# Hash attention with adapters: the sum of v written once per head and added by VectorE

## The chip, the cores and the metric

The kernel runs on one core of one Trainium2 chip. Its metric is the device time of one execution in microseconds (us). The parts of the core that matter here are TensorE (PE, with PEld for its weight loads), VectorE (DVE), ScalarE (ACT), GpSimd (POOL) and the DMA queue that SyncE (SP) issues.

## The reference

Four batches of eight heads, 768 positions, head size 64. Queries and keys are hashed to six sign bits each; a key takes part for a query only where the two hashes agree. The heads' outputs, side by side, are 3072 rows of 512, on which a mixture of eight rank-16 adapters works.

```python
q_bits = (np.einsum('bhsd,dk->bhsk', q, proj) > 0)      # k likewise
mask = q_bucket[:, :, :, None] == k_bucket[:, :, None, :]
scores = np.where(mask, scale * q @ k.T, -1e9)          # scale = 1/8
attn = softmax(scores)                                  # no key agrees: all weights equal
x = (attn @ v)                                          # [4*768, 8*64]
logits = x @ w_gate                                     # two largest of 8 experts, softmax of these
out = x + sum over the two of w * (x @ A[e]) @ B[e]
```

Where no key agrees, softmax gives every key the same weight, so the output is the mean of v.

## The kernel before

The 32 heads are handled as 16 pairs (p = 0 to 15; two heads h). For each pair:

- q, k and v are loaded by SP (`load_q`, `load_k`, L176; `load_v`, L184) in natural layout, 128 partitions with six positions each.
- Hashes: VectorE turns 32x32 blocks (`turn32`, L212), TensorE multiplies by the hash weights (`hash`, L222), VectorE takes signs (`sign`, L231), and the signs go out to DRAM and come back as rows 64 to 71 of the tile aug (`sign_out`, L238; `sign_in`, L244).
- q and k proper: GpSimd scales and casts to bf16 (`natcast`, L252), a transposing DMA writes them into aug (`cross`, L259), and the second head's half is moved to the first partitions by VectorE for q and by GpSimd for k (`shift_v`, `shift_p`, L267).
- Scores: `s0` to `s8` (L365) are nine blocks of 1024 columns, keys in the partitions. The hash rows make scores of keys that don't agree so small that their exponential vanishes. There are three score banks (`ps_s`, `bufs=3`). ScalarE takes the exponential of each block (`x0` to `x8`, L371), 144 in all.
- Values: for each head, `p00` to `p05` and `p10` to `p15` (`pvk`, L384) multiply the exponentials by v with a column of ones beside it, into one bank (`ps_v`, `bufs=1`): six query tiles of 65 columns, the 65th being the sum of the weights. Ahead of them `u0` and `u1` (`uni`, L376) write the sum of v over all keys, multiplied by 2^-56, into all six tiles at once, 390 columns. This is the case in which no key agrees: beside real weights it is too small to count. GpSimd makes the sums of v over a partition's six positions in three steps (`vsum0` to `vsum2`, L200, L203, L205), the matmul sums over partitions.
- `norm0` and `norm1` (L401, L403): VectorE takes the reciprocal of each tile's 65th column and multiplies the 64 others by it, from the bank into x. When it has done so the bank is free for the next head.

Per batch (four pairs) x is cast (`to_bf`, POOL, L412), turned by TensorE (`turn`, L421), copied (`xcopy`, DVE, L426), and multiplied by the gate and the A matrices (`lz`, L443; copy `lzc`, DVE, L447); routing (`route`, `exp`, `gate`, `inv`) is small work on VectorE and ScalarE (L459 to L485), the products with the gate are on GpSimd (`prod`, L492), then come a turn (`zt`, `ztc`), the product with B (`d`, L518), the sum (`sum`, DVE, L536) and the store (`st`). Hashes, turns, gates and deltas share a single bank "m" (`ps_m`, `bufs=1`), so each of them waits until the one before has been copied out.

All orders are written out by hand: `PLAN` holds a row of steps for each pair, and every engine and the DMA queue executes its instructions in the order in which the steps stand. A step's suffix is the pair it belongs to, relative to the row: `hash+2` works ahead for a later pair, `norm1-1` finishes the pair before. In row 0 the first pair has special steps for its shorter start (`order`, `tr`, `copy`, `cast`, `hash`, `sign` by halves). The last two pairs are finished by other functions (`uni3`, `pv3`, `norm3`; steps with A to F), with their own broadcast matmul (L812).

Of the kernel before, what the change touches and what calls it, by code (L numbers as in the profile page):

```python
# [13 lines left out]
F32 = mybir.dt.float32  # L14
BF16 = mybir.dt.bfloat16
AX = mybir.AxisListType
ALU = mybir.AluOpType
# [3 lines left out]
class Emitter:  # L21
    def __init__(self, ctx, tc, q, k, v, proj, w_gate, A, Bm, out):
        self.tc, self.nc = tc, tc.nc
        self.q, self.k, self.v, self.out = q, k, v, out
        B, H, S, D = q.shape
# [38 lines left out]
        self.vs3, self.vs1, self.ps = {}, {}, {}  # L64
# [129 lines left out]
    def vsum(self, p, k):  # L194

        nc, T, D = self.nc, self.T, self.D
        vn, vb = self.vn[p], self.vb[p % 3]
        if k == 0:
            s3 = self.vs3[p] = self.vsp.tile([self.P, 2, 3, D], F32, tag="vs3", name=f"vs3_{p}")
            nc.gpsimd.tensor_add(out=s3, in0=vn[:, :, 0:3, :], in1=vn[:, :, 3:6, :])  # L200
        elif k == 1:
            s1 = self.vs1[p] = self.vsp.tile([self.P, 2, D], F32, tag="vs1", name=f"vs1_{p}")
            nc.gpsimd.tensor_add(out=s1, in0=self.vs3[p][:, :, 0, :], in1=self.vs3[p][:, :, 1, :])  # L203
        else:
            nc.gpsimd.tensor_add(out=vb[:, :, T, 0:D], in0=self.vs1[p], in1=self.vs3[p][:, :, 2, :])  # L205
# [167 lines left out]
    def uni(self, p, h):  # L373
        T, D = self.T, self.D
        pv = self.pv[p, h] = self.ps_v.tile([self.P, T, D + 1], F32, tag="v", name=f"pv{p}_{h}")
        self.nc.tensor.matmul(out=pv, lhsT=self.eps,  # L376
                              rhs=self.vb[p % 3][:, h, T:T + 1, :].to_broadcast([self.P, T, D + 1]),
                              start=True, stop=False, skip_group_check=True)
# [14 lines left out]
    def norm(self, p, h):  # L393
# [5 lines left out]
        pv = self.pv[p, h]  # L399
        ri = self.smallp.tile([P, T], F32, tag="ri", name=f"ri{p}_{h}")  # L400
# [290 lines left out]
    def step(self, token, p):  # L691
# [21 lines left out]

# [4 lines left out]

# [4 lines left out]

# [4 lines left out]

# [6 lines left out]

# [5 lines left out]

# [5 lines left out]

# [5 lines left out]

# [4 lines left out]

# [5 lines left out]

# [5 lines left out]

# [4 lines left out]

# [143 lines left out]
```

## Time and profile before

| what | us |
| --- | --- |
| runs | 160.62, 161.14, 164.03; median 161.14 |
| profiled execution, its own time | 161.96 |
| its span | 160.0 |
| PE busy / weight loads | 149.8 / 106.4 |
| ACT busy, of which the 144 exponentials | 140.1 / 134.2 |
| DVE busy | 115.1 |
| POOL busy | 109.0 |
| first exponential starts, last ends | 10.9, 148.4 |

The profile comes from one execution, whose own time lies between the runs; the span is what its instructions cover. Busy time of an engine is time in which at least one of its instructions runs, so instructions that overlap count once. A stretch A:B lies between two times from the span's start; its row gives the busy time of each engine, with the number of instructions in brackets, then the granted TensorE clock, the DMA share and GB/s. In a row of a group the figures behind the count are the busy time of all, the mean of one in ns, and the idle time of the engine before them with what ended it. In the order of time a row has its start, its length and what it is.

### The profile page before, as it was taken

What the parts mean: (1) busy time and instruction counts of PE and PEld (TensorE: products, weight loads), DVE (VectorE), ACT (ScalarE), POOL (GpSimd) and SP (SyncE); (2) the same over time, 40 slices, a digit from 0 to 9 for tenths busy, and PEclk for the clock granted to TensorE, in tenths of its full rate; (3) what the DMA queues carried; (4) which work ended last, traced back from release to release, by engine and by line L of the source; (5) the groups of instructions that cost most, each with busy time, mean ns of one, the idle gap of its engine ahead of it and who ended that gap; (6) DMA issues with size and microseconds to landing.
All of it is one profiled execution on the core that took longest, in us unless ns stands there. A gap on an engine that the chain in (4) does not pass through costs nothing.

```text
span 160.0 us, 5374 instructions
## 1 busy us (share of the span) xinstructions
PE 149.8 (94%) x2188; PEld 106.4 (66%) x2188; DVE 115.1 (72%) x316; ACT 140.1 (88%) x164; POOL 109.0 (68%) x180
## 2 busy tenths in 40 slices
PE   7999899999999999999999999999999999999730
PEld 4655566767676577666767776666777688899400
DVE  4488866477374779967768997778796777778861
ACT  3149989999999899999999999999999999998440
POOL 3489887975896947999989559996769359100360
PEclk9999999999999999999999999999999999999996
DMA  5898998989989989998989989899975552223146
GB/s 137 260 336 236 204 227 199 266 169 265 200 91 296 169 169 319 294 192 204 267 261 264 286 195 234 223 213 249 277 219 103 158 214 106 94 90 132 46 177 216
DMA packets 57552, 33.03 MB, mean 206 GB/s; under 512 B 42552, under 2 KB 55608, under 8 KB 57528
## 3 DMA queue, kind: packets, MB, share of 16 engines
q1 hardware_dynamic: 57304, 32.56, 82.3%
q8 instruction: 17, 0.28, 0.8%
q10 hardware_dynamic: 224, 0.13, 0.3%
q14 instruction: 7, 0.06, 0.1%
HBM read 20.15 MB, written 7.03 MB: 170 GB/s over the span
## 4 chain that ended last, share of the span: by engine, by line
PE 70%; DMA 15%; SPq 5%; DVE 3%; ACT 2%; issue 1%; POOL 1%; DVEq 0%; POOLq 0%
PE s L365 28%; PE pv L384 13%; DMA aug<-nb 11%; PE hs L222 5%; DMA nat<-in_k_dram 4%; PE lz L443 3%; PE pvl L822 3%; PE dl L518 2%; PE xtp L421 2%; PE pv L376 2%; SPq L147 2%; PE hb L582 2%; PE s L315 2%; PE xt L845 1%; ACT P L371 1%
## 5 line engine op out<-in xcount | busy, mean ns | idle before, releaser
L371 ACT ACTIVATE P<-s 128x1024 bf16<-128x1024 f32 x144 | 134.2, 1072 | 4.8 <-PE s L365 2.4
L365 PE MATMUL s<-aug 71*128 71x256 bf16 (+3 forms) x396 | 76.7, 311 | 0.2 <-DMA aug<-dr 0.2
L384 PEld LDWEIGHTS <-P 128*128 128x128 bf16 x1008 | 40.3, 98 | 9.1 <-issue 0.5
L384 PE MATMUL pv<-vb,P 128*128 128x65 bf16 x1008 | 43.4, 193 | 0.0
L365 PEld LDWEIGHTS <-aug 71*128 71x128 bf16 x396 | 31.9, 97 | 14.5 <-issue 3.3
L212 DVE STREAM_TRANSPOSE R<-nat 128x768 f32<-128x768 f32 x30 | 28.9, 968 | 1.8 <-DMA nat<-in_k_dram 1.6
L252 POOL TENSOR_SCALAR nb<-nat 128x768 bf16<-128x768 f32 x30 | 24.9, 831 | 2.5
L492 POOL TENSOR_TENSOR zm<-lzs,gw 128x128 bf16<-128x128 f32 x22 | 8.3, 402 | 20.3 <-DVE gw L478 18.2
L200 POOL TENSOR_TENSOR vs<-vn 128x384 f32<-128x384 f32 x16 | 16.0, 998 | 2.2 <-DMA vn<-in_v_dram 1.8
L536 DVE SCALAR_TENSOR_TENSOR acc<-dl,rt,x 128x512 f32<-128x512 f32 x18 | 13.4, 744 | 5.2 <-PE dl L518 5.2
L403 DVE TENSOR_TENSOR x<-pv,ri 128x384 f32<-128x384 f32 x28 | 15.6, 557 | 1.0
L412 POOL CAST xb<-x 128x768 bf16<-128x768 f32 x14 | 11.5, 824 | 6.4 <-DVE x L403 6.2
L267 POOL COPY aug<-aug 64x768 bf16<-64x768 bf16 x14 | 11.8, 843 | 4.4 <-DMA aug<-nb 3.8
L222 PE MATMUL hs<-R,hst 128*32 128x192 f32 x240 | 13.8, 332 | 0.2 <-DVE R L212 0.2
L192 POOL CAST vb<-vn 128x768 bf16<-128x768 f32 x16 | 13.4, 836 | 0.8 <-DMA vn<-in_v_dram 0.7
L401 DVE RECIPROCAL ri<-pv 128x6 f32<-128x6 f32 x28 | 5.3, 189 | 7.9 <-PE pv L384 7.5
L267 DVE COPY aug<-aug 64x768 bf16<-64x768 bf16 x14 | 8.8, 627 | 2.5 <-DMA aug<-nb 2.1
L222 PEld LDWEIGHTS hs<-R,hst 128*32 128x32 f32 x240 | 6.5, 109 | 5.4 <-DVE ri L401 1.8
L231 DVE TENSOR_SCALAR s<-hs,soff 128x192 bf16<-128x192 f32 x15 | 6.1, 410 | 5.0 <-PE hs L222 5.0
L443 PE MATMUL lz<-wa,xT 128*128 128x136 bf16 x96 | 9.5, 222 | 0.2 <-DVE xT L850 0.2
L376 PE MATMUL pv<-vb,eps 128*128 128x390 bf16 x28 | 9.3, 333 | 0.3 <-DVE aug L568 0.3
L426 DVE COPY xT<-xtp 128x768 bf16<-128x768 bf16 x14 | 7.7, 552 | 1.9 <-PE xtp L421 1.9
(98 smaller groups left out, 153.8 us busy)
## 6 DMA issues: line engine op xcount, KB each, us to landing
vn<-in_v_dram SPq DMA_DIRECT2D x16, 384.0 KB
nat<-in_q_dram SPq DMA_DIRECT2D x15, 384.0 KB
nat<-in_k_dram SPq DMA_DIRECT2D x15, 384.0 KB
out_dram<-acc SPq DMA_DIRECT2D x9, 512.0 KB
out_dram<-acc SPq DMA_DIRECT2D x5, 256.0 KB
dr<-s SPq DMA_DIRECT2D x15, 48.0 KB
aug<-dr SPq DMA_DIRECT2D x15, 48.0 KB
nat<-in_q_dram SPq DMA_DIRECT2D x2, 192.0 KB
```

The source lines that it names most:

```text
L192: nc.gpsimd.tensor_copy(out=vb[:, :, 0:T, 0:D], in_=vn)
L200: nc.gpsimd.tensor_add(out=s3, in0=vn[:, :, 0:3, :], in1=vn[:, :, 3:6, :])
L212: self.nc.vector.transpose(out=self.R[p][:, i], in_=self.nat[p][:, i])
L222: nc.tensor.matmul(out=self.hs[p][32 * j:32 * j + 32], lhsT=self.hst[:, hf].rearrange("p b i -> p (b i)"), rhs=rhs, start=(hf == 0), stop= ...
L252: self.nc.gpsimd.tensor_scalar(out=self.nb[p][:, :, i].rearrange("p t h d -> p h t d"), in0=self.nat[p][:, i].rearrange("p h (t d) -> p h ...
L267: (self.nc.gpsimd if i else self.nc.vector).tensor_copy(out=aug[0:64, :, i, 1, :], in_=aug[64:128, :, i, 0, :])
L365: nc.tensor.matmul(out=ps[:, c - lo:c - lo + n * P], lhsT=aug[0:71, kt, 1, h, :], rhs=aug[0:71, q:q + n, 0, h, :], start=True, stop=True)
L371: self.nc.scalar.activation(out=self.P_[p][:, lo:lo + 1024], in_=ps, func=ACT.Exp, scale=128.0)
L384: self.nc.tensor.matmul(out=pv[:, i, :], lhsT=self.P_[w][:, o:o + self.P], rhs=vb[:, h, kt, :], start=False, stop=(kt == self.T - 1), skip ...
L403: nc.vector.tensor_tensor(out=self.x[b][:, :, c:c + D], in0=pv[:, :, 0:D], in1=ri.unsqueeze(2).to_broadcast([P, T, D]), op=ALU.mult)
L443: nc.tensor.matmul(out=ps, lhsT=self.xT[b][:, t, i, :], rhs=self.wa[:, t, :], start=(t == 0 and (keep or i == I[0])), stop=(t == self.nD - ...
L536: nc.vector.scalar_tensor_tensor(out=acc, in0=ps, scalar=rt, in1=x, op0=ALU.mult, op1=ALU.add)
```

## The change

`uni` writes the scaled sum of v only once, as a seventh tile of 65 columns in the bank. `norm` copies these 65 columns to SBUF (um), adds them to the six tiles with one VectorE instruction into an SBUF tile (w), and takes reciprocal and multiply from that tile. The second step of the sum of v works in place. All 16 rows of `PLAN` differ; of these the first and two of the middle are shown.

```diff
@@ vsum
         elif k == 1:
-            s1 = self.vs1[p] = self.vsp.tile([self.P, 2, D], F32, tag="vs1", name=f"vs1_{p}")
-            nc.gpsimd.tensor_add(out=s1, in0=self.vs3[p][:, :, 0, :], in1=self.vs3[p][:, :, 1, :])
+            s3 = self.vs3[p]
+            nc.gpsimd.tensor_add(out=s3[:, :, 0, :], in0=s3[:, :, 0, :], in1=s3[:, :, 1, :])
         else:
-            nc.gpsimd.tensor_add(out=vb[:, :, T, 0:D], in0=self.vs1[p], in1=self.vs3[p][:, :, 2, :])
+            nc.gpsimd.tensor_add(out=vb[:, :, T, 0:D], in0=self.vs3[p][:, :, 0, :], in1=self.vs3[p][:, :, 2, :])
@@ uni
-        pv = self.pv[p, h] = self.ps_v.tile([self.P, T, D + 1], F32, tag="v", name=f"pv{p}_{h}")
-        self.nc.tensor.matmul(out=pv, lhsT=self.eps,
-                              rhs=self.vb[p % 3][:, h, T:T + 1, :].to_broadcast([self.P, T, D + 1]),
-                              start=True, stop=False, skip_group_check=True)
+        pv = self.pv[p, h] = self.ps_v.tile([self.P, T + 1, D + 1], F32, tag="v", name=f"pv{p}_{h}")
+        self.nc.tensor.matmul(out=pv[:, T, :], lhsT=self.eps, rhs=self.vb[p % 3][:, h, T, :],
+                              start=True, stop=True, skip_group_check=True)
@@ norm
         pv = self.pv[p, h]
+        um = self.smallp.tile([P, 1, D + 1], F32, tag="um", name=f"um{p}_{h}")
+        nc.vector.tensor_copy(out=um, in_=pv[:, T:T + 1, :])
+        w = self.vsp.tile([P, T, D + 1], F32, tag="pvs", name=f"pvs{p}_{h}")
+        nc.vector.tensor_tensor(out=w, in0=pv[:, 0:T, :], in1=um.to_broadcast([P, T, D + 1]), op=ALU.add)
+        pv = w
         ri = self.smallp.tile([P, T], F32, tag="ri", name=f"ri{p}_{h}")
         nc.vector.reciprocal(out=ri, in_=pv[:, :, D])
@@ PLAN, row 0
-        "order_q0 tr_q0 order_k0 copy_q0 tr_k0 warm4 proj_second order_k1 cast_q0 hash_q0 copy_k0 hash_k0 "
-        "load_q+1 order_q1 load_k+1 sign_q0 tr_q1 cast_k0 load_v sign_k0 copy_q1 tr_k1 copy_k1 load_q+2 "
-        "hash_q1 proj_groups turn32_q+1 cast_q1 hash_weights cast_k1 natcast_q+1 hash_k1 load_k+2 vcast "
-        "sign_q1 turn32_k+1 natcast_q+2 sign_k1 s0 natcast_k+1 s1 hash+1 s2 natcast_k+2 x0 sign+1 "
+        "order_q0 order_k0 tr_q0 copy_q0 tr_k0 cast_q0 load_q+1 proj_second copy_k0 hash_q0 hash_k0 "
+        "order_k1 sign_k0 load_k+1 order_q1 proj_groups cast_k0 sign_q0 tr_k1 copy_k1 tr_q1 hash_k1 "
+        "hash_weights copy_q1 natcast_q+1 hash_q1 load_k+2 load_q+3 cast_k1 s0 turn32_q+1 natcast_k+2 "
+        "sign_k1 sign_q1 x0 s1 cast_q1 load_v turn32_k+1 x1 s2 natcast_k+1 hash+1 load_q+2 t1q s3 sign+1 "
+        "load_k+3 turn32_k+2 q1q0 q1q1 x2 vcast s5 turn32_q+2 warm4 natcast_q+2 t1k vsum0 s4 x3 q1k1 s6 "
...
@@ PLAN, rows 5 and 6, new
+        "s0 lzc1:0 norm0-1 hash+2 sign+2 u1-1 p10-1 p11-1 x7-1 s1 shift_v+1 lz0:0 x0 x8-1 vsum2 lzc0:0 "
+        "p12-1 x1 p13-1 load_q+3 route0:0 p14-1 vsum0+1 p15-1 vsum1+1 exp0:0 lz3:0 s2 s3 vcast+1 "
+        "shift_p+1 s4 cross+2 lzc3:0 x2 norm1-1 u0 lz4:0 p00 lzc4:0 x3 p01 p02 sign_in+1 lz5:0 s5 "
+        "load_k+3 lzc5:0 to_bf-1 route1:0 s6 x4 shift_v+2 load_moe:5 exp1:0 gate1:0 gate0:0 x5 x6 turn-1 "
+        "p03 p04 sign_out+2 prod2:0 s7 prod0:0 inv1:0 p05 prod1:0 inv0:0 vsum2+1 load_k+4 x7 s8 xcopy-1 "
+        "load_v+2 norm0 x8",
+        "s0 zt0:0 load_q+3 u1-1 s1 cast_moe:5 ztc0:0 shift_p+1 d0:0 p10-1 load_v+2 sign_in+1 turn32_q+2 "
+        "x1 sum0:0 turn32_k+2 p11-1 p12-1 p13-1 s2 x0 p14-1 p15-1 x2 load_k+4 natcast_q+2 s3 natcast_k+2 "
+        "prod5:0 s4 prod3:0 cross+2 norm1-1 vcast+1 x3 hash+2 s5 natcast_k+3 u0 p00 p01 x4 prod4:0 p02 "
+        "natcast_q+3 sign+2 vsum0+1 turn32_q+3 d2:0 sum2:0 s6 turn32_k+3 s7 p03 d1:0 x5 s8 sign_out+2 "
+        "sum1:0 p04 p05 norm0 to_bf-1 x6",
```

More of the change, by code (lines that the diff above doesn't have):

```diff
@@ L63, in __init__ @@
         self.zm, self.zT, self.rt, self.acc, self.rg = {}, {}, {}, {}, {}
-        self.vs3, self.vs1, self.ps = {}, {}, {}
+        self.vs3, self.ps = {}, {}
         self.pend, self.at = {}, {}
```

146 rows, old and new, of the table PLAN are left out of this document.

## The prediction

> **What bounds the kernel now.** I read the page's first part, then a table of busy time by stretch, cut at the pairs of heads: before the first exponential, pairs 0 to 4, pairs 5 to 13, pairs 14 and 15, and the end behind the last exponential.
>
> ```profile
> span 160.0 us, 5374 instructions
> PE 149.8 (94%) x2188; PEld 106.4 (66%) x2188; DVE 115.1 (72%) x316; ACT 140.1 (88%) x164; POOL 109.0 (68%) x180
> ...
> core 0: us, PE busy (x) PEld busy (x) DVE busy (x) ACT busy (x) POOL busy (x), PEclk, DMA share, GB/s
> 0.00:10.90 10.90, 9.54 (x48) 6.05 (x50) 5.82 (x26) 2.82 (x5) 5.70 (x28) 1.00 0.77 232
> 10.90:54.63 43.73, 42.73 (x655) 28.53 (x652) 28.93 (x53) 41.85 (x45) 35.86 (x52) 1.00 1.03 215
> 54.63:130.40 75.77, 75.77 (x1159) 54.20 (x1158) 60.23 (x166) 75.23 (x86) 59.27 (x88) 1.00 0.92 224
> 130.40:148.42 18.02, 18.02 (x309) 15.72 (x306) 13.91 (x48) 17.35 (x21) 4.82 (x10) 1.00 0.35 139
> 148.42:160.00 11.58, 3.76 (x32) 1.89 (x30) 6.25 (x26) 2.87 (x9) 3.35 (x5) 0.87 0.38 138
> ```
>
> The shares of the whole span would name PE. The stretches say more: between 10.90 and 148.42 us ScalarE (ACT) is as full as PE, 75.23 of 75.77 us in the longest one. VectorE (DVE) has 60.23 there, the only compute engine with real room beside GpSimd (POOL). Next, how regular the exponentials are, from the order of time on ACT:
>
> ```profile
> 10.90 1.94 ACT L371 ACTIVATE P<-s 128x1024 bf16<-128x1024 f32 x2 [1.81 <-PE s L315]
> ...
> 20.45 8.39 ACT L371 ACTIVATE P<-s 128x1024 bf16<-128x1024 f32 x9 [0.80 <-PE s L365]
> ...
> 61.43 11.10 ACT L371 ACTIVATE P<-s 128x1024 bf16<-128x1024 f32 x12
> ```
>
> Twelve exponentials in a row take 11.10 us and one lasts 1.07 us (the group's row below), so they start (11.10 − 1.07)/11 = 0.91 us apart. All 144 at that pace need 143 × 0.91 + 1.07 = 131.2 us; they took 148.42 − 10.90 = 137.5. So the exponentials set a floor, and no relief of another engine can win back more than about 6 us between them. PE is level with ACT, and the score banks (three of them) let it run about two exponentials, 1.8 us, ahead.
>
> The Trainium skill says the same against reading PE's 94% as the bound: "Trainium Kernel Development and Optimization", section Performance Expectations, calls matmul busy time a bad measure because matmuls are pipelined and takes the weight loads' share for a better one. Here that is PEld's 66%.
>
> **The change part by part.** The prices come from the groups kept apart by shape (busy us, mean ns of one, then the idle time before them).
>
> ```profile
> L371 ACT ACTIVATE P<-s 128x1024 bf16<-128x1024 f32 x144 | 134.2, 1072 | 4.8 <-PE s L365 2.4 <-PE s L315 2.0
> L376 PE MATMUL pv<-vb,eps 128*128 128x390 bf16 x28 | 9.3, 333 | 0.3 <-DVE aug L568 0.3
> L812 PE MATMUL pvl<-vb,eps 128*128 128x65 bf16 x4 | 0.4, 193 | 0.0
> L403 DVE TENSOR_TENSOR x<-pv,ri 128x384 f32<-128x384 f32 x28 | 15.6, 557 | 1.0
> L401 DVE RECIPROCAL ri<-pv 128x6 f32<-128x6 f32 x28 | 5.3, 189 | 7.9 <-PE pv L384 7.5
> L447 DVE COPY lzs<-lz 128x136 f32<-128x136 f32 x18 | 5.3, 294 | 5.0 <-PE lz L443 4.9
> L459 DVE MAX8 top<-lzs 128x8 f32<-128x8 f32 x23 | 2.3, 155 | 0.1
> L485 DVE RECIPROCAL rt<-ss 128x3 f32<-128x3 f32 x7 | 1.2, 169 | 0.1
> L267 DVE COPY aug<-aug 64x768 bf16<-64x768 bf16 x14 | 8.8, 627 | 2.5 <-DMA aug<-nb 2.1
> L203 POOL TENSOR_TENSOR vs<-vs 128x128 f32<-128x128 f32 x16 | 7.3, 455 | 1.2
> ```
>
> *PE, removed.* The 390-column matmul with the small weights becomes one of 65 columns. That form stands in the trace (L812): 193 ns against 333. So 28 × 0.14 = 3.9 us of PE go. In the long stretch ACT is as full, so this buys slack, not time; in all I credit 0.5 us (bounds 0 and 3.9).
>
> *DVE, added.* Each of 28 head steps gets a copy of 65 columns and an addition of 390 before the reciprocal. The copy lies between L485's 169 ns (3 elements) and L447's 294 (136 columns): 0.22. The addition is L403's shape with six more elements: 0.56. Two instructions that depend on each other stand about 0.04 apart:
>
> ```profile
> 21.55 0.18 DVE L401 RECIPROCAL ri<-pv 128x6 f32<-128x6 f32 x1
> 21.77 0.56 DVE L403 TENSOR_TENSOR x<-pv,ri 128x384 f32<-128x384 f32 x1
> ```
>
> (21.55 + 0.18 = 21.73, and the multiply starts at 21.77.) So a head step costs 0.22 + 0.56 + 2 × 0.03 to 0.04 = 0.84 us more; at the ends, 0.17 + 0.56 + 0.06 = 0.79 and 0.30 + 0.56 + 0.08 = 0.94. The bank of a head is held no longer than now: copy and addition, 0.82 us, stand where reciprocal and multiply, 0.78, stood. Reciprocal and multiply now run behind the release, but on the same engine.
>
> *The multiply changes its place of reading.* It read the matmul's bank and ri; now both inputs lie in SBUF. The trace shows what such instructions meet when POOL works:
>
> ```profile
> 26.66 0.82 POOL L267 COPY aug<-aug 64x768 bf16<-64x768 bf16 x1 [0.81 <-DMA aug<-nb]
> 26.67 1.03 DVE L267 COPY aug<-aug 64x768 bf16<-64x768 bf16 x1
> ...
> 59.49 0.35 DVE L267 COPY aug<-aug 64x768 bf16<-64x768 bf16 x1
> ...
> 93.70 0.22 DVE L478 SCALAR_TENSOR_TENSOR gw<-lzs,top,e 128x8 f32<-128x8 f32 x1
> ...
> 93.85 0.44 DVE L478 SCALAR_TENSOR_TENSOR gw<-lzs,top,e 128x8 f32<-128x8 f32 x1
> 93.87 0.40 POOL L492 TENSOR_TENSOR zm<-lzs,gw 128x128 bf16<-128x128 f32 x1 [0.20 <-DVE gw L478]
> ```
>
> The same DVE copy took 0.35 us while POOL stood idle and 1.03 beside a POOL instruction that started 10 ns earlier: it ended 0.22 us behind it. The gate instruction (L478), with two tensor inputs in SBUF, took 0.22 us alone and 0.44 beside POOL's product. Over its 14 instances the copy averages 627 ns, 0.27 us above 0.35. I take 0.27 us for each multiply as well; the bounds are nothing (POOL never in the way) and 0.8 (a whole POOL instruction ahead). With it a head step costs 0.84 + 0.27 = 1.11 us more, 28 of them 31 us.
>
> The Trainium skill has the rule: "SBUF — State Buffer", section Who interferes with whom, says a VectorE instruction with two SBUF inputs contends with a GpSimd instruction that reads SBUF, whichever starts first keeping the shared ports to its end. The copy at 26.67 agrees for its kind. A reader who trusts only the opposite, that the multiply never waits, gets 0.84 per step.
>
> *What the sum is where it falls.* In the new lists rows 5 to 13 hold 19 head steps against 17 in the old; a head step costs 0.78 now. So DVE needs 60.23 + 2 × 0.78 + 19 × 1.11 = 82.9 us where the stretch lasts 75.77. Part of a busy figure overlaps when DVE is crowded: two transposes of 0.97 us fit in 1.91 (below), 0.03 less; the 23 maxima (L459) of 155 ns are busy 2.3 us together, 0.05 less on each. At 0.04 us on each of the 166 instructions, an estimate, 6.6 us go and 76.3 are left.
>
> ```profile
> 15.11 1.91 DVE L212 STREAM_TRANSPOSE R<-nat 128x768 f32<-128x768 f32 x2
> ...
> 88.22:96.86 8.64, 8.64 (x131) 6.28 (x130) 8.31 (x35) 8.56 (x12) 5.11 (x10) 1.00 0.94 248
> ```
>
> The most crowded pair of the old kernel had DVE busy for 8.31 of 8.64 us (96%). With every gap closed the stretch takes 76.3 us, +0.5; with 82.9 at 96% it takes 86.4, +10.6. I take the middle, **+5.5 us**. What queues behind a late multiply is everything DVE does for PE's one shared bank "m": signs (L231), turned copies (L426), gate copies (L447) and sums (L536). PE executes in order, so a hash, turn or delta that waits for that bank holds the next scores, and 1.8 us later ACT is idle.
>
> Pairs 0 to 4 have room: 28.93 + 8 × 1.11 = 37.8 of 43.73 us, though rows 1 and 2 of the new lists crowd; +0.5. Pairs 14 and 15 finish through the other helper (uni3, norm3), which is untouched, and the end as well: 0.
>
> *The first row of steps.* Four warming matmuls move from ahead of the first scores to behind the sixth, and the casts of the second halves are rearranged. The first exponential may come up to 0.9 us earlier. But pair 1 starts when its signs have gone out to DRAM and back:
>
> ```profile
> 12.52 0.42 DVE L231 TENSOR_SCALAR s<-hs,soff 128x192 bf16<-128x192 f32 x1 [0.45 <-PE hs L222]
> 12.96 0.37 SPq L238 DMA_DIRECT2D dr<-s  x1
> ...
> 16.66 0.34 SPq L244 DMA_DIRECT2D aug<-dr  x1
> ...
> 19.80 1.09 PEld L365 LDWEIGHTS <-aug 71*128 71x128 bf16 x8 [0.37 <-DMA aug<-dr]
> ```
>
> Sign at 12.52, out at 12.96, in at 16.66, first scores at 19.80: 7.3 us. In the new list pair 1's second transpose stands behind both late signs of pair 0, so this chain does not start earlier. An earlier first exponential waits longer at 20.45 (it waits 0.80 there already). I count 0, bounds −0.8 and +0.8. The queue of SP issues the same transfers in another order; nat loads behind nat3's buffer push v's first load later, which is wanted only at the end of pair 0: 0. The in-place sum of v replaces L203 by an instruction of the same shape, 455 ns: 0, on POOL.
>
> Sum against the profiled execution's own 161.96 us (span 160.0): +5.5 + 0.5 − 0.5 = 167.5. That run was 0.8 above the median of the runs shown, 161.14, so the forecast for the median is **166.5 us**.
>
> **The rivals.** *A, DVE becomes the bound (above):* 166.5. Against it: its average share is only 72% now.
>
> *B, DVE still fits.* If the overlap reaches its 6.6 us and POOL is seldom in the way, DVE ends level with ACT, and PE's slack returns a part of the 6 us that the exponentials lose. Time: 161.1 − 1.6 to +2.5, so 159.5 to 163.6. For it: the lists could place head steps into the slack of rows 4, 7 and 11.
>
> *C, PE was the bound after all.* Then all of 3.9 us comes off, 157.2. For it: 75.77 of 75.77 busy; against it: ACT's 75.23 in the same stretch, and the head steps' 31 us.
>
> *D, POOL is drawn in.* The skill's page named above has the lock work both ways. As a mechanism of this kernel: each multiply keeps a POOL instruction waiting for up to 0.56 us, 19 × 0.56 = 10.6 us on POOL's 59.27 of 75.77, which fits, but late natcasts delay the transposing DMA and so the scores of later pairs. At the upper bound, +10.6 and 1 more in pairs 0 to 4: 172.7.
>
> *E, the change does not do what it says:* the 65-column matmul saves less than 0.14 us (a fixed cost). Then A without 0.5: 167; I count it to A.
>
> **How the numbers follow.** A 0.55, D 0.13, B 0.25, C 0.07. The time is A's, 166.5. The range reaches over B's lower end to D's upper one: 159.5 to 173. What a measurement of this kernel can tell from no change is about 2%, that is 157.9 to 164.4. Slower: A nearly whole (0.53) and D, 0.66. Within 2%: B and the rest of A, 0.27. Faster: C, 0.07.
>
> **What would show it.** DVE busy at 140 us or more, near full from pair 5 to 13; the multiply's mean above 0.7 us with single ones near 1.2; waits of PE's weight loads and of ACT growing behind DVE; the eps matmul at 193 ns. The forecast is wrong if the multiply keeps 0.56 us beside POOL, if ACT still starts an exponential every 0.91 us through pairs 5 to 13, or if the new order of transfers costs more than the arithmetic.

## The result

The changed kernel takes 171.66 us (median; 169.91 to 176.58) against 162.58 for the kernel before beside it. The ratio is 1.058, 95% interval 1.048 to 1.067; like every ratio below it leaves out executions that the chip ran in a slower state; here it compares 170.38 and 169.91 us with 161.14 and 160.62. In a second comparison it was 1.051 (1.035 to 1.067). The forecast of 166.5 us had the direction and the engine right, and the size a good deal too small. The profiled execution took 170.38 us, its span is 168.4.

The page's first part of the changed kernel, and its table by stretch, cut at the same places in the work (first exponential, pair 5, pair 14, last exponential, end):

```profile
PE 151.1 (90%) x2187; PEld 104.6 (62%) x2188; DVE 135.6 (81%) x372; ACT 142.4 (85%) x164; POOL 113.9 (68%) x180
```

```profile
0.00:10.76 10.76, 8.95 (x44) 5.08 (x46) 5.19 (x25) 2.93 (x6) 5.50 (x27) 1.00 0.67 198
10.76:56.27 45.51, 42.01 (x666) 28.16 (x661) 35.29 (x71) 42.34 (x45) 38.38 (x55) 1.00 1.11 223
56.27:138.89 82.62, 78.44 (x1171) 54.22 (x1168) 74.85 (x208) 77.01 (x88) 61.33 (x86) 0.98 0.80 203
138.89:156.90 18.01, 17.95 (x295) 15.26 (x291) 14.06 (x46) 17.27 (x20) 5.35 (x10) 1.00 0.33 131
156.90:168.40 11.50, 3.76 (x32) 1.92 (x31) 6.22 (x26) 2.87 (x8) 3.36 (x5) 0.86 0.38 140
```

The columns are those of the table before: length of the stretch, then PE, PEld, DVE, ACT, POOL. Of the 8.4 us that the span grew, 6.85 lie in pairs 5 to 13 (82.62 against 75.77) and 1.78 in pairs 0 to 4 (45.51 against 43.73); the other three stretches are 0.2 shorter together. In the long stretch ACT was busy for all but 0.5 us and is now idle for 5.6; DVE went from 60.23 to 74.85, 91% of the stretch.

The groups of the changed kernel that answer to those priced in the prediction (now `norm` has lines 402, 404, 407 and 409, the small matmul line 378):

```profile
L371 ACT ACTIVATE P<-s 128x1024 bf16<-128x1024 f32 x144 | 135.7, 1034 | 10.2 <-PE s L365 6.1 <-PE s L315 3.3
L409 DVE TENSOR_TENSOR x<-pvs,ri 128x384 f32<-128x384 f32 x28 | 21.0, 749 | 1.0
L404 DVE TENSOR_TENSOR pvs<-pv,um 128x390 f32<-128x390 f32 x28 | 15.8, 565 | 1.0
L402 DVE COPY um<-pv 128x65 f32<-128x65 f32 x28 | 6.0, 216 | 7.4 <-PE pv L385 7.3
L267 DVE COPY aug<-aug 64x768 bf16<-64x768 bf16 x14 | 6.0, 425 | 0.4
L378 PE MATMUL pv<-vb,eps 128*128 128x65 bf16 x28 | 5.5, 198 | 1.4 <-POOL vb L205 0.8 <-POOL vs L200 0.2 <-DVE pvs L404 0.2
L407 DVE RECIPROCAL ri<-pvs 128x6 f32<-128x6 f32 x28 | 5.4, 193 | 0.9
```

Copy 216 ns and addition 565 are the forecast's 0.22 and 0.56. The multiply rose from 557 to 749 ns, 0.19 more, where 0.27 was taken. Its spread shows why (durations in ns: least, median, most):

```profile
L409 DVE TENSOR_TENSOR x<-pvs,ri x28: 557/640/1197, 22.8 to 141.3; 128x384 f32<-128x384 f32 x28
```

At best it is the old 557, at worst it waits for 0.64 us. In the order of time on VectorE and POOL, 8 of the 28 keep 557 to 560 ns, and each of the other 20 ends 0.40 to 0.42 us behind the end of a POOL instruction that was running when it started. The exponentials' waits for scores of pairs 1 onward (L365) grew from 2.4 to 6.1 us.

### The profile page after: what moved, and what is told of

Read it like the earlier page. It is cut to its first block, busy times and chain, and to the rows that moved or that the text cites. A ratio compares the mean times of both kernels' runs of the same rounds, so it can differ in the third digit from the quotient of the medians.

```text
span 168.4 us, 5427 instructions
## 1 busy us (share of the span) xinstructions
PE 151.1 (90%) x2187; PEld 104.6 (62%) x2188; DVE 135.6 (81%) x372; ACT 142.4 (85%) x164; POOL 113.9 (68%) x180
## 5 line engine op out<-in xcount | busy, mean ns | idle before, releaser
L371 ACT ACTIVATE P<-s 128x1024 bf16<-128x1024 f32 x144 | 135.7, 1034 | 10.2 <-PE s L365 6.1
L365 PE MATMUL s<-aug 71*128 71x256 bf16 (+3 forms) x396 | 75.2, 313 | 0.8 <-DMA aug<-dr 0.5
L385 PEld LDWEIGHTS <-P 128*128 128x128 bf16 x1008 | 39.3, 99 | 7.2 <-issue 2.2
L365 PEld LDWEIGHTS <-aug 71*128 71x128 bf16 x396 | 31.9, 98 | 14.9 <-issue 3.5
L498 POOL TENSOR_TENSOR zm<-lzs,gw 128x128 bf16<-128x128 f32 x22 | 9.3, 439 | 21.5 <-DVE gw L484 18.0
L409 DVE TENSOR_TENSOR x<-pvs,ri 128x384 f32<-128x384 f32 x28 | 21.0, 749 | 1.0
L200 POOL TENSOR_TENSOR vs<-vn 128x384 f32<-128x384 f32 x16 | 16.6, 1037 | 0.2
L404 DVE TENSOR_TENSOR pvs<-pv,um 128x390 f32<-128x390 f32 x28 | 15.8, 565 | 1.0
L267 POOL COPY aug<-aug 64x768 bf16<-64x768 bf16 x14 | 12.8, 914 | 0.9
L402 DVE COPY um<-pv 128x65 f32<-128x65 f32 x28 | 6.0, 216 | 7.4 <-PE pv L385 7.3
L449 PEld LDWEIGHTS <-xT 128*128 128x128 bf16 x96 | 6.9, 97 | 3.7 <-issue 2.0
L524 PE MATMUL dl<-Bcat,zT 128*128 128x512 bf16 x18 | 7.0, 390 | 1.9 <-DVE s L231 1.1
```

Of the source, the lines that this page charges most:

```text
L365: nc.tensor.matmul(out=ps[:, c - lo:c - lo + n * P], lhsT=aug[0:71, kt, 1, h, :], rhs=aug[0:71, q:q + n, 0, h, :], start=True, stop=True)
L371: self.nc.scalar.activation(out=self.P_[p][:, lo:lo + 1024], in_=ps, func=ACT.Exp, scale=128.0)
L385: self.nc.tensor.matmul(out=pv[:, i, :], lhsT=self.P_[w][:, o:o + self.P], rhs=vb[:, h, kt, :], start=False, stop=(kt == self.T - 1), skip ...
L404: nc.vector.tensor_tensor(out=w, in0=pv[:, 0:T, :], in1=um.to_broadcast([P, T, D + 1]), op=ALU.add)
L409: nc.vector.tensor_tensor(out=self.x[b][:, :, c:c + D], in0=pv[:, :, 0:D], in1=ri.unsqueeze(2).to_broadcast([P, T, D]), op=ALU.mult)
L449: nc.tensor.matmul(out=ps, lhsT=self.xT[b][:, t, i, :], rhs=self.wa[:, t, :], start=(t == 0 and (keep or i == I[0])), stop=(t == self.nD - ...
```

## The experiments

Theory: the time of VectorE in pairs 5 to 13 is what the change costs. Rivals: the new step lists and their transfers; waiting for POOL at the shared reads; the hold of the only value bank; a late x. Ratios are to the kernel before, run beside each. The edits are shown shortened, with remarks in brackets or behind a #.

**Lists alone, arithmetic alone.** The old `uni` and `norm` in the new lists:

```diff
-    PLAN = (old rows)
+    PLAN = (the changed kernel's rows)
```

> The old arithmetic (broadcast matmul of 390 columns, reciprocal and multiply from the bank) in the new step lists. Theory (DVE's added 20 us are the cause): the lists cost little by themselves, so 158 to 165 us, DVE busy near 115, the multiply's mean at 0.56. Rival (the new lists themselves are worse, through the order of transfers and steps): 167 us or more with DVE still at 115.

164.93 us, ratio 1.014 (1.007 to 1.020), at the top of the expected band; VectorE is busy for 113.3 us. And the new `uni`, `norm` and `vsum` in the old lists:

```diff
-        pv = self.pv[p, h] = self.ps_v.tile([self.P, T, D + 1], ...)
+        pv = self.pv[p, h] = self.ps_v.tile([self.P, T + 1, D + 1], ...)
...
+        nc.vector.tensor_copy(out=um, in_=pv[:, T:T + 1, :])
+        nc.vector.tensor_tensor(out=w, in0=pv[:, 0:T, :], in1=um.to_broadcast([P, T, D + 1]), op=ALU.add)
```

> The new arithmetic (65 columns, copy, add, multiply from SBUF) in the old step lists. Theory: as slow as the changed kernel or slower, 168 to 178 us, because the old lists leave no room for the longer head steps; DVE busy near 135. Rival (the lists are the cause): 160 to 164.

176.03 us, ratio 1.089 (1.084 to 1.094). So the arithmetic is the cause, and the new lists are not a second one: beside the new arithmetic they win back some 3 of 9 per cent, for the old arithmetic they are 1.4% worse than the old ones.

**PE's relief without VectorE's load.** In the new lists:

```diff
-        um = ...; nc.vector.tensor_copy(...); w = ...; nc.vector.tensor_tensor(...); pv = w
+        pv = pv[:, 0:T, :]
```

> The changed kernel without the copy and the addition: the sum of v is still written once, but not added, so queries with no agreeing key lose their mean of v. Reciprocal and multiply read the bank. It holds all of PE's relief and none of VectorE's load. Theory: 157 to 162 us, DVE near 114, multiply 0.56. If PE's 3.9 us were worth their full amount, 157 or less; if lists and transfers were the cause, 166 or more.

162.78 us, 0.8 above the expected band, ratio 1.008 (1.004 to 1.012). The same edit with the old lists:

> The old step lists and the 65-column matmul, without copy and addition (queries with no agreeing key lose their mean of v). It differs from the kernel before only in 28 shorter matmuls. If ScalarE's pace sets the time, as the prediction has it: within 1% of before, 160 to 162.5 us. If PE was the bound: 156 to 158.

161.91 us, ratio 0.997 (0.991 to 1.002). Both kernels leave the addition out. So the 28 shorter matmuls are worth nothing that can be measured in either order, and without VectorE's added work the slowdown is gone.

**Bank and shared reads.** The sum is written back into the bank, and the multiply reads it there:

```diff
-        w = self.vsp.tile([P, T, D + 1], F32, tag="pvs", name=f"pvs{p}_{h}")
+        w = pv[:, 0:T, :]
```

> The changed kernel with the sum written back into the bank, so that the multiply again has one input in PSUM; the bank is held until the multiply ends, 0.75 us longer. Theory that waiting for POOL is a large part: multiply back at 0.56, DVE busy near 130, and 1 to 3 us faster than the changed kernel. Rival (only the copy and the addition count, and the longer hold of the bank costs as much): the same time or slower.

173.54 us, ratio 1.078 (1.072 to 1.083): slower than the changed kernel, as the rival had it, though the multiply is back at a mean of 557 ns and VectorE is busy for 131.7 us instead of 135.6. Its list of waits (us in total, times, longest) shows the price:

```profile
PE pv L378 <- DVE x L409: 11.4, 18, 1.1
PEld L378 <- DVE x L409: 11.1, 14, 1.3
ACT P L371 <- PE s L365: 9.8, 23, 0.9
```

The next head's first matmul (L378) now waits for the multiply. To tell the longer hold from the writing to the bank, the changed kernel with a small read of the bank behind its multiply:

```diff
+        rd = self.smallp.tile([P, 1, 8], F32, tag="rd", name=f"rd{p}_{h}")
+        nc.vector.tensor_copy(out=rd, in_=bank[:, T:T + 1, 0:8])
```

> The changed kernel with one more small read of the bank behind the multiply, which holds the bank until then: about 1.9 us instead of 0.8. VectorE's load is that of the changed kernel and 28 small copies. Theory (the hold of the only value bank is what made the sum in the bank slower): 174 to 179 us. Rival (writing the sum into the bank was slow by itself): 171 to 173.

181.5 us, ratio 1.112 (1.104 to 1.121), beyond the expected band. The small copies are 4.4 us of work for VectorE too, but the first matmul of the next head now waits 16.6 us in all for them. So the hold of the value bank is expensive, and it was right for the change to release it after 0.8 us. It is not what the change pays for: in the changed kernel L378 waits for the addition (L404), which releases the bank, for 2.3 us in all.

**Where.** The old arithmetic for pairs 5 to 13 only, and for pairs 0 to 4 only, in the new lists:

```diff
+        if 5 <= p <= 13:      # in the other run: if not 5 <= p <= 13
+            (old uni and norm)
+        else:
+            (new uni and norm)
```

> The changed kernel with the old arithmetic for pairs 5 to 13 and the new for pairs 0 to 4. Theory (the time goes where VectorE is crowded): 165 to 168 us, with the exponentials of pairs 5 to 13 losing 3 to 4 us against an even pace instead of 9.4. Rival (the loss comes from anywhere, by the number of head steps): 18 of 28 steps recover two thirds of the difference to the lists alone, 167 to 168.5, and pairs 0 to 4 lose as much per step as the others did.

> The opposite: the old arithmetic for pairs 0 to 4, the new for pairs 5 to 13. Theory: 169 to 171 us, the loss in pairs 5 to 13 stays near 9. Rival (by the number of steps): 166.5 to 168.

164.82 us, ratio 1.017 (1.011 to 1.023), and 171.19 us, ratio 1.055 (1.049 to 1.062), each 0.2 us outside its expected band. The intervals of the first and of the lists alone overlap, and so do those of the second and of the whole change. The ten head steps of pairs 0 to 4 cost nothing that can be told, the eighteen of pairs 5 to 13 everything that can. In pairs 0 to 4 of the changed kernel VectorE is busy for 35.29 of 45.51 us, 78%; there it has room.

**VectorE's time as such.** The old arithmetic in the new lists, with work that nobody reads behind the multiply, when the bank is already free:

```diff
+        for n in range(2):      # with a third fill: range(3)
+            w = self.vsp.tile([P, T, D + 1], F32, tag="pvs", name=...)
+            nc.vector.memset(w, 0.0)
```

> The old arithmetic in the new lists with two fills of 390 columns behind each head's multiply, which nobody reads: VectorE gets about 0.9 us more per head step, as in the changed kernel, but the bank is not held longer, nothing reads two inputs from SBUF, and PE has no relief. Theory (VectorE's time as such): 168 to 173 us, DVE busy near 137. Rival (the time is lost through waiting for POOL or the bank, and spare VectorE time would absorb the rest): 164 to 166.

165.08 us, ratio 1.019 (1.015 to 1.024). This hit the rival: 16 us more on VectorE, and hardly a change against the lists alone. But a fill took only 0.38 us, so that VectorE was busy for 129.5 us and not for the 137 that were meant; the changed kernel has 135.6. Three things stayed open, and three more kernels took one each. With an instruction that reads two inputs from SBUF:

```diff
+        nc.vector.memset(w, 0.0)
+        nc.vector.tensor_tensor(out=w2, in0=self.ident[:, 0:65] (broadcast), in1=self.projW[:, 0:65] (broadcast), op=ALU.mult)
```

> The old arithmetic in the new lists; behind each head's multiply one fill and one multiply of 390 columns with two inputs in SBUF that nobody reads. The bank is released and x is written before them. Theory P (meeting POOL at the shared reads is what costs): 168 to 171 us, POOL's own instructions longer by 3 us or more in all. Rival X (the later x): 164 to 166. Rival L (VectorE's last microseconds of load): as e13.

168.08 us, ratio 1.041 (1.029 to 1.052), the lower edge of theory P's band. With x written late:

```diff
+        (two fills)
+        nc.vector.reciprocal(out=y, in_=self.x[b][:, 0:1, c:c + 1])
+        nc.vector.reciprocal(out=self.x[b][:, 0:1, c:c + 1], in_=y)
```

> The old arithmetic in the new lists with two fills behind the multiply and then two tiny reciprocals that rewrite one column of x (1/(1/x), the same value but for rounding), so that x counts as written 1.1 us later while the bank is released as before and no instruction has two inputs in SBUF. Theory X (x is late for the cast on POOL, which holds the steps behind it): 168 to 171 us, with POOL waiting longer for x. Rival P (meeting POOL): 164.5 to 166.5.

167.75 us, ratio 1.037 (1.027 to 1.046), between the two bands. With a third fill:

> As e9_load with three fills instead of two, so VectorE is busy about as long as in the changed kernel or a little longer (137 us). Theory L (VectorE has a limit near there and the time goes up steeply behind it): 168 to 171 us. Rivals P and X: 165 to 166.5.

172.26 us, ratio 1.063 (1.055 to 1.072), above the band of theory L, with VectorE busy for 139.6 us. The third fill costs 7 us where the first two cost nothing that can be told. The rows of pairs 5 to 13 put these runs into one order. The first is the lists alone, then two fills:

```profile
54.57:131.51 76.94, 76.67 (x1172) 54.28 (x1169) 59.49 (x170) 75.81 (x89) 57.57 (x85) 1.00 0.89 218
```

```profile
56.16:133.94 77.78, 77.14 (x1173) 54.26 (x1171) 69.79 (x208) 76.29 (x88) 58.01 (x85) 1.00 0.86 219
```

two inputs from SBUF, then late x:

```profile
56.21:136.04 79.83, 77.85 (x1173) 54.45 (x1171) 73.29 (x208) 76.69 (x89) 66.23 (x86) 1.00 0.85 214
```

```profile
54.91:135.60 80.69, 78.84 (x1173) 54.41 (x1171) 73.48 (x246) 76.86 (x88) 58.31 (x86) 1.00 0.84 211
```

three fills, and then the new arithmetic in pairs 5 to 13 only:

```profile
55.59:139.46 83.87, 79.58 (x1173) 54.33 (x1171) 76.75 (x226) 77.28 (x88) 58.10 (x86) 1.00 0.79 203
```

```profile
56.25:140.21 83.96, 79.66 (x1174) 55.29 (x1172) 74.16 (x205) 76.98 (x88) 60.54 (x85) 0.96 0.77 200
```

| kernel, pairs 5 to 13 | DVE busy | length | DVE share |
| --- | --- | --- | --- |
| lists alone | 59.5 | 76.9 | 77% |
| two fills | 69.8 | 77.8 | 90% |
| two inputs | 73.3 | 79.8 | 92% |
| late x | 73.5 | 80.7 | 91% |
| the change | 74.9 | 82.6 | 91% |
| the change, executed again (below) | 74.5 | 81.8 | 91% |
| three fills | 76.8 | 83.9 | 92% |
| new arithmetic in these pairs only | 74.2 | 84.0 | 88% |
| new arithmetic, old lists | 75.3 | 86.9 | 87% |
| sum in the bank | 72.0 | 83.6 | 86% |
| bank held | 77.0 | 89.9 | 86% |

Up to about 70 us of work VectorE takes what it is given, and the stretch stays as long as ScalarE makes it (busy for 76.3 of 77.8 us with two fills). From two fills to three, 7.0 us more work make it 6.1 us longer. On the straight line between these two, the work of the changed kernel (74.85) gives 82.2 us; it took 82.62, and its second execution 81.8 where the line gives 81.9. That is within what two executions of one kernel differ by, so VectorE's work alone is enough to account for the length. The last four rows lie 2.4, 4.3, 3.8 and 5.8 us above that line: the old lists and a longer hold of the bank cost time beside VectorE's work, and so does something in the first of the four (see the clock). So 91 or 92% is what the new lists reach at best, with the bank released early, and not shown to be a bound of the engine. Of the 7.8 us in which VectorE stands idle in the changed kernel's stretch, 4.6 are waits for PE's results (x times the gate and A matrices 1.6, turned x 1.4, values 1.1, a delta 0.5); the rest are gaps of less than 0.15 us between its instructions.

Two inputs and late x, with equal work, lie 1.0 and 0.3 us below the line. So meeting POOL counts through the time that it adds to VectorE, and neither it nor the late x shows a cost beside that. That POOL is slowed too is seen in the two pages' first parts, two inputs and late x:

```profile
PE 151.5 (91%) x2188; PEld 105.5 (64%) x2188; DVE 133.7 (81%) x372; ACT 142.2 (86%) x164; POOL 120.2 (73%) x180
```

```profile
PE 152.0 (92%) x2188; PEld 105.4 (64%) x2188; DVE 134.2 (81%) x428; ACT 142.0 (86%) x164; POOL 109.6 (66%) x180
```

Ten us more on POOL cost the kernel nothing that shows here. The Trainium skill's "SBUF — State Buffer", section Who interferes with whom, has the lock work in both directions; these runs agree, with 0.64 us as the longest wait of a multiply in the changed kernel and 10.6 us more in total on POOL in the run with two inputs than in that with late x.

**The clock.** The changed kernel's long stretch has a mean granted clock of 0.98. Its rows by microsecond (last three columns: granted clock, DMA share, GB/s):

```profile
65.00:66.00 1.00, 0.53 (x2) 0.03 (x1) 1.00 (x2) 1.00 (x2) 0.94 (x2) 1.00 1.00 350
66.00:67.00 1.00, 0.81 (x9) 0.54 (x10) 1.00 (x3) 1.00 (x2) 0.91 (x2) 0.63 1.05 390
67.00:68.00 1.00, 1.00 (x21) 1.00 (x19) 1.00 (x3) 0.63 (x1) 0.92 (x2) 0.50 0.71 243
68.00:69.00 1.00, 1.00 (x10) 0.59 (x8) 0.54 (x1) 0.02 (x1) 0.92 (x3) 0.50 0.89 191
```

The order of time on VectorE, POOL and PE says how it came about:

```profile
64.85 0.61 POOL L160 CAST Bcat<-Bf 128x512 bf16<-128x512 f32 x1
...
64.93 0.94 DVE L409 TENSOR_TENSOR x<-pvs,ri 128x384 f32<-128x384 f32 x1
65.79 0.35 DVE L514 COPY zT<-ztp 128x384 bf16<-128x384 bf16 x1
...
66.19 0.58 PE L524 MATMUL dl<-Bcat,zT 128*128 128x512 bf16 x1 [0.67 <-DVE zT L514]
```

A multiply ends 0.41 us behind a cast on POOL, the copy behind it is late, and PE, in order, waits 0.67 us for it. At 66.26 us, just behind this wait, its granted clock falls to half, until 69.68. One delta was moved behind four value steps, so that PE has work there:

```diff
-  ... shift_p+1 d0:0 p10-1 load_v+2 sign_in+1 turn32_q+2 x1 sum0:0 turn32_k+2 p11-1 p12-1 p13-1 s2 ...
+  ... shift_p+1 p10-1 load_v+2 sign_in+1 turn32_q+2 p11-1 p12-1 p13-1 d0:0 x1 sum0:0 turn32_k+2 s2 ...
```

> The changed kernel with one delta matmul of batch 0 (row 6) moved behind four of the value steps of pair 5, so that PE has work while VectorE is late with the turned gate products at 66 us. If PE's idle time there is what lowered its granted clock to half for 3.4 us, the clock stays full between 60 and 80 us and the time falls by 1 to 2.5 us against the changed kernel. If the lowering has another cause, it comes at the same place or close by and the time stays within 0.5 us.

170.65 us, ratio 1.053 (1.041 to 1.065), with the changed kernel again beside it:

> The changed kernel again beside it on the same chip: 170 to 172 us, PE's clock at half for some 3.4 us near 66 us again if the lowering belongs to this order of work, elsewhere or not at all if it does not.

171.92 us, ratio 1.051 (1.035 to 1.067), its clock at half for 3.4 us again in the same pair (pair 6), from 69.08 us on. The edit did what it was for, as the row of the same moment in its profile shows:

```profile
66.00:67.00 1.00, 1.00 (x26) 0.86 (x24) 1.00 (x3) 1.00 (x2) 0.94 (x2) 1.00 1.07 389
```

The clock stays full, and no gain in time can be told: the ratios are 1.053 and 1.051, and the medians differ by less than their intervals, which are too wide to rule out 1 us. But the stretch of pairs 5 to 13 is 82.48 us against 82.62 and 81.81, with VectorE still at 92%:

```profile
56.82:139.30 82.48, 77.68 (x1170) 53.46 (x1167) 75.91 (x208) 76.79 (x88) 60.77 (x85) 1.00 0.83 205
```

By the starts of its exponentials, pair 6 took 8.7 us instead of 10.2, and pairs 5 and 7 together 1.2 us more. So the slow clock in this place comes from VectorE's lateness, and what PE gained without it was lost again in the pairs beside it. That a low clock never costs time is not shown: in the run with the new arithmetic in pairs 5 to 13 only, it fell twice, and the second time, in pair 11, that pair took 12.4 us where the changed kernel took 10.2. Which of the two caused the other was not tested. No version tried is faster than the kernel before.

## Why the prediction was right or wrong

- *ScalarE is as full as PE, so PE's relief buys no time.* Right, and more so than put: the credit of 0.5 us should have been 0 (ratio 0.997, 0.991 to 1.002, in the old lists). Rival C falls with it.
- *The price of a head step.* Copy, addition and gaps as forecast; the multiply's wait 0.19 instead of 0.27 us. Together 1.03 instead of 1.11.
- *The bank is released no later.* Right; the two runs that hold it longer are another 2 and 5 per cent slower.
- *VectorE becomes the bound in pairs 5 to 13.* Right in the sense that from about 90% on the stretch grows with its work, shown by the place (old arithmetic there: 1.017; elsewhere: 1.055) and by the fills. Rival B, that VectorE's work still fits, falls with it.
- *Rival D, POOL is drawn in.* Its time, 172.7, came nearer than the forecast's, but not by its path. POOL's work in the long stretch rose by 2.1 us (61.33 for 59.27), not by 10.6, and the run that did put 10.6 us more on POOL lies below the line of the fills.
- **The step that failed** is the end of the sum for that stretch, where the length was worked out from VectorE's work, as the middle between +0.5 and +10.6 us. It has two halves.
  - The demand was put at 82.9 us gross and 76.3 with overlap; 74.85 came. The stretch holds 18 head steps in both profiles, not 17 and 19 (those were counted in the rows of the lists): 2.7 us too much. The ten copies of L267 in it got 2.0 us cheaper (4.4 for 6.4). Against that, the 6.6 us of overlap were too many: the busy time of before has 6.7 us of overlap taken off already (its instructions there last 67.0 us together, and it is busy for 60.2), and after has only 2.1 us more (83.7 and 74.9).
  - How full VectorE can be was put between 96 and 100%, from the most crowded pair of the old kernel. Over nine pairs it is 91%, in both executions of the change; 74.85 us at 96% would be 78.0, and 82.6 came.
  - The first error made the demand too high, the second the length too short. That +5.5 lies only 1.4 below +6.85 (0.5 below the +6.0 of the second execution) is luck.
- *Pairs 0 to 4: +0.5.* Also too small: +1.8, and +3.9 in the second execution of the same kernel (47.7 us). It is not clearly the arithmetic: with the old arithmetic in these pairs (the run with the new in 5 to 13) they took 46.3 us, with the new (the run with the old in 5 to 13) 45.5, and the lists alone took 44.7. In pair 0 the exponentials wait three times for L315 (3.3 us for 2.0 before), and natcasts now stand between the casts on POOL that the first scores need; that the one comes from the other is not shown. What sets this stretch, beyond a spread of some 2 us between executions, the runs do not settle.
- *The first row of steps: 0.* Nearly so: the first exponential comes 0.14 us earlier and pair 1 starts 0.34 us later, at 20.79. In the lists alone the first exponential came 0.98 us earlier, at 9.92, and pair 1 still started at 20.77, which fits the chain of the signs.
- *The step from the profiled run to the median.* 0.8 us were taken off, as the profiled run of before lay above its median, and 0.1 by rounding; the profiled run of after lies 1.3 below its own. That is 2.2 of the 5.2 us by which the median exceeds the forecast. The long stretch makes 1.4, pairs 0 to 4 make 1.3 and the credit for PE 0.5, and the other stretches take back 0.2.

Of what was to show it, the multiply's mean (749 ns) with single ones near 1.2 us, the small matmul (198 ns for 193) and the longer waits of the exponentials came true. VectorE's 140 us did not (135.6), and "near full" was 91%.

## What to carry to other kernels

Where several engines are level, work moved from one to another is worth the relief of the first only if that one sets the pace, and costs nothing on the second only up to a point. That point is to be read stretch by stretch, and it can lie well below 100% of busy time: here, with orders written by hand and single banks, it lay near 90%, and from there 7.0 us of work added 6.1 us. Freeing a scarce bank early was worth a copy here; making the later work read two inputs from SBUF beside a busy GpSimd put a wait into its price. And a forecast from single profiles needs the spread between executions: one stretch of the same kernel differed by 2.2 us between two.

## What the runs showed of the hardware

PE's granted clock fell to half for 3.4 us after PE had been idle for less than a microsecond: the row at 66.19 has 0.67 us of idle time, and the clock was already down in part of 66.00 to 67.00. With work put into that pause it stayed full. The Trainium skill's "TensorE: Matmul & The Clock Gate", Part 1, names an idle window of about 3.4 us as what lowers it; here a much shorter pause in a thinly filled stretch was enough, and the measurement decides. The length of the lowered time, 3.4 us, agrees.

VectorE's bf16 copies between partitions (L267), which nobody had changed, went from 627 to 425 ns in the mean, and to 503, 600, 395 and 534 in the runs with two fills, two inputs, late x and three fills. At its shortest such a copy takes 0.355 us. In the order of time of before, 9 of the 14 were longer, of after 5, and each of these ended 0.21 to 0.22 us behind a POOL instruction that was running when it started. The multiply with two inputs in SBUF ended 0.40 to 0.42 us behind one. So the price of an instruction that can meet POOL depends on where the others push it, here by about as much as the multiply's own wait.
